# W2 = KV·Wo from full 128x128 array passes with a masked KV, plainer normalization, and four DMAs issued from ScalarE's queue

## The chip, the cores and the metric

The kernel runs on one core of a Trainium2 chip. The metric is device time in microseconds (us). TensorE (PE in the profile, with PEld for its weight loads) does the matrix products, VectorE (DVE) and ScalarE (ACT) empty PSUM and do the elementwise work, GpSimd (POOL) builds masks, and SyncE (SP) issues the DMAs. A DMA is issued from the instruction queue of one engine, and 16 DMA engines carry the data.

## The reference

The input x has 2048 rows of 1024 (bf16). Two attention blocks with 32 heads of 32 columns run on the same x, and a gate mixes them.

- Gate: g = sigmoid(sum of x * gate_w over a row).
- Block A is linear attention: q, k, v = x @ wqkv; phi(t) = (t + 1 where t > 0, else exp(t)) + 1e-6; per head KV = phi(k)^T v (32x32), z = the column sums of phi(k), and o = (phi(q) KV) / (phi(q)·z + 1e-6); a = o @ wo.
- Block B is sliding-window attention: eight keys per query at distance 0, 2, ..., 14, softmax over them, then @ its own wo.
- Output: g * a + (1 - g) * b.

## The kernel before, in words

Rows are handled in 16 tiles of 128 (`NB`), the 1024 columns in eight slabs of 128 (`KT`). TensorE's order is written out by hand for the whole kernel, VectorE's for the first stage; the other queues follow the order in which the code issues.

**Start.** SyncE issues, in this order: the DMA transpose of row tile 0 of x into `xT` (L95), the first two quarters of the weight half `WkA[0]` (L99, 256 KB each, slabs 0-1 and 2-3), the transpose of row tile 1 (L98), quarters three and four (L99), then 14 more transposes (L102) and the bulk loads of further weights and of x by rows. ScalarE's first instruction is the load of its activation table (L70). TensorE spins 36 small warm-up products (L158), then takes tile 0 with slabs 0-3, tile 1 with slabs 0-3, tile 0 with 4-5, tile 1 with 4-5, and so on, each as its quarter lands (L152).

**Stage 1.** pk = phi(x Wk) for 16 tiles and two column halves (L152, 256 products). Then G = x^T pk (L200, 256 products), so that KV^T = Wv^T G can be had without ever forming v (L220). L220 makes the transposed 64x64 diagonal blocks in pairs: array tiles 128x64, two side by side, 128 products of 64 columns; two bank-sized results are copied into `KVT`, which is 128 x 8 x 64. Only the 32x32 head blocks in it are used.

**W2 and V.** Next KV is folded into Wo, W2 = KV·Wo, in place in `WoA`. `w2_event(g, half)` (L246) uses the array as 32x32 tiles: 16 products of 512 columns, one per head of half g, into four banks, emptied by VectorE and ScalarE two each (L250). A bank then holds four heads that are four apart, so that the rows of W2 come out in a permuted head order. The four events are interleaved with the 64 products of the first four V tiles of block B (`v_units`, L258) at places 8, 20, 32 and 44. PSUM pool `ps_1` has six banks, which KV, W2, V and Q share in rotation.

**V and Q of block A.** Twelve rounds of 16 V products (L258) and 16 Q products of block A (L296). `qa_finish` applies phi and `normalize`: product with z (L277), sum per head (L279), + 1e-6 (L281), reciprocal (L282), times `ratio` (L284), and two multiplications of 512 columns that write the result in the same permuted head order as W2's rows (L286). The result goes to DRAM (`pqd`) and comes back transposed later.

**Stage 2** is block B: K and Q projections (L339) with scores (L365) and weighted sums (L390) interleaved. **Stage 3** multiplies: for each row tile, 8 slabs of normalized phi(q) with W2 and 8 slabs of block B's output with its Wo accumulate in one bank (L454); ScalarE scales it by 1 - g (`omg`, L459; W2's side carries the factor `ratio` = g/(1 - g)) and SyncE stores it (L461). Row tiles 12-15 are normalized late (`qa_late`), from `raw` into a tile of their own, `lw`. The last row tile is written in three parts of 512, 256 and 256 columns.

Of the kernel before, what the change touches and what calls it, by code (L numbers as in the profile page):

```python
# [9 lines left out]
ALU = mybir.AluOpType  # L10
BF16 = mybir.dt.bfloat16
F32 = mybir.dt.float32
PE = mybir.EngineType.PE
DVE = mybir.EngineType.DVE
P = 128
# [14 lines left out]
def interleave(units, events):  # L30

    events = sorted(events, key=lambda e: e[0])
    for i, unit in enumerate(units):
        while events and events[0][0] <= i:
            events.pop(0)[1]()
        unit()
    for _, fn in events:
        fn()
# [3 lines left out]
def kernel(  # L42
# [11 lines left out]
    nc = tc.nc  # L54
    S, D = A_x.shape[1:]
# [3 lines left out]
    out2 = out[0].rearrange("(m two) d -> two m d", two=2)  # L59

    def rows(ap, s0, s1):
        return ap[s0 // 1024, s0 % 1024:(s1 - 1) % 1024 + 1, :]

    H = 32
    Dh = D // H
    KT = D // P
    NB = S // P
# [4 lines left out]
    consts = ctx.enter_context(tc.tile_pool(name="consts", bufs=1))  # L72
    wpool = ctx.enter_context(tc.tile_pool(name="wpool", bufs=2))
# [20 lines left out]
    WkA = [wpool.tile([P, KT, 512], BF16, name="WkA0", tag="wa")]  # L94
    nc.sync.dma_start_transpose(out=xT[:, :, 0:P], in_=rows(x, 0, P))  # L95
    for i in range(4):
        if i == 2:
            nc.sync.dma_start_transpose(out=xT[:, :, P:2 * P], in_=rows(x, P, 2 * P))  # L98
        nc.sync.dma_start(out=WkA[0][:, 2 * i:2 * i + 2, :],  # L99
                          in_=A_wqkv[2 * i * P:(2 * i + 2) * P, D:D + 512].rearrange("(kt p) n -> p kt n", p=P))  # L100
    for t in range(2, NB):
        nc.sync.dma_start_transpose(out=xT[:, :, t * P:(t + 1) * P], in_=rows(x, t * P, (t + 1) * P))  # L102
    WkA += load_w("WkA", A_wqkv, D, "wa", only=(1,))
# [3 lines left out]
    WvA = load_w("WvA", A_wqkv, 2 * D, "wb")  # L107
    WoA = load_w("WoA", A_wo, 0, "wo")
# [3 lines left out]

    onesb = consts.tile([P, P], BF16, name="onesb")
    nc.vector.memset(onesb[:], 1.0)


    def band(dst, lead):
# [11 lines left out]
    ratio = consts.tile([P, NB], F32, name="ratio")  # L129
    omg = consts.tile([P, NB], F32, name="omg")  # L130
    zrow = consts.tile([P, D], F32, name="zrow")
    KVT = consts.tile([P, KT, 64], BF16, name="KVT")

    work = ctx.enter_context(tc.tile_pool(name="work", bufs=3))
    small3 = ctx.enter_context(tc.tile_pool(name="small3", bufs=2))
# [7 lines left out]
    with tc.manual_schedule(engines={PE}):  # L143

        with ExitStack() as s1:
            ps_1 = s1.enter_context(tc.tile_pool(name="ps_1", bufs=6, space=bass.MemoryType.PSUM))
# [37 lines left out]
            for t in range(1, NB):  # L184
                side.append(lambda t=t: nc.vector.tensor_tensor(
                    out=zacc[:], in0=zacc[:] if t > 1 else pk[:, 0, :], in1=pk[:, t, :], op=ALU.add))
            side.append(lambda: nc.gpsimd.partition_all_reduce(zrow[:], zacc[:], P, bass_isa.ReduceOp.add))
            for t in range(NB):
                side.append(lambda t=t: nc.vector.tensor_tensor_reduce(
                    out=gjunk[:], in0=xrow[:, t, :], in1=gw_row[:], scale=1.0, scalar=0.0, op0=ALU.mult,  # L190
                    op1=ALU.add, accum_out=gdot[:, t:t + 1]))

            G = []
            for half in range(2):
                g_ = kq.tile([P, KT, 512], BF16, name=f"G{half}", tag="kq")
                G.append(g_)
                for kt in range(KT):
                    pj = ps_1.tile([P, 512], F32, name="g_ps", tag="p1")
                    for t in range(NB):
                        nc.tensor.matmul(pj[:], lhsT=xrow[:, t, kt * P:(kt + 1) * P],  # L200
                                         rhs=pk[:, t, half * 512:(half + 1) * 512],
                                         start=(t == 0), stop=(t == NB - 1))
# [7 lines left out]
            nc.vector.tensor_scalar(out=omg[:], in0=ratio[:], scalar1=1.0, scalar2=None, op0=ALU.add)  # L210
            nc.vector.reciprocal(out=omg[:], in_=omg[:])


            for g in range(2):
                kvp = ps_1.tile([P, 4, 64], F32, name="kv_ps", tag="p1")
                for c in range(4):
                    for kt in range(KT):
                        for j in range(2):
                            cols = slice(c * P + 64 * j, c * P + 64 * j + 64)
                            nc.tensor.matmul(kvp[64 * j:64 * j + 64, c, :], lhsT=WvA[g][:, kt, cols],  # L220
                                             rhs=G[g][:, kt, cols], start=(kt == 0), stop=(kt == KT - 1))
                nc.vector.tensor_copy(out=KVT[:, 4 * g:4 * g + 4, :], in_=kvp[:])
            WkB = load_w("WkB", B_wqkv, D, "wb")


# [9 lines left out]
            def bank1():  # L235
                return ps_1.tile([P, 512], F32, name="p1_ps", tag="p1")

            def w2_event(g, half):  # L240
                def go():
                    w2p = [bank1() for _ in range(4)]
                    for j in range(4):
                        for r in range(4):
                            rs = slice(32 * r, 32 * r + 32)
                            nc.tensor.matmul(w2p[r][32 * j:32 * j + 32, :],  # L246
                                             lhsT=KVT[rs, 4 * g + j, (r % 2) * 32:(r % 2) * 32 + 32],
                                             rhs=WoA[half][rs, 4 * g + j, :], start=True, stop=True)
                    for r in range(4):
                        (nc.scalar.copy if r % 2 else nc.vector.tensor_copy)(  # L250
                            out=WoA[half][:, 4 * g + r, :], in_=w2p[r][:])
                return go

            def v_units(t):
# [21 lines left out]
            def normalize(t, pq, pn, prod):  # L276
                nc.vector.tensor_tensor(out=prod, in0=pq, in1=zrow[:], op=ALU.mult)  # L277
                den = small3.tile([P, H], F32, name="den", tag="den")
                nc.vector.tensor_reduce(out=den[:], in_=prod.rearrange("p (h e) -> p h e", h=H),  # L279
                                        axis=mybir.AxisListType.X, op=ALU.add)  # L280
                nc.vector.tensor_scalar(out=den[:], in0=den[:], scalar1=1e-6, scalar2=None, op0=ALU.add)  # L281
                nc.vector.reciprocal(out=den[:], in_=den[:])  # L282

                nc.vector.tensor_scalar(out=den[:], in0=den[:], scalar1=ratio[:, t:t + 1], scalar2=None, op0=ALU.mult)  # L284
                for g in range(2):
                    nc.vector.tensor_tensor(  # L286
                        out=pn[:, 512 * g:512 * g + 512].rearrange("p (r j e) -> p j r e", r=4, j=4),
                        in0=pq[:, 512 * g:512 * g + 512].rearrange("p (j r e) -> p j r e", r=4, j=4),
                        in1=den[:, 16 * g:16 * g + 16].rearrange("p (j r o) -> p j r o", r=4, o=1)
                        .broadcast_to([P, 4, 4, Dh]), op=ALU.mult)  # L290

            def qa_units(t, bank, evacuate):
                def mm(half, kt, st):
# [16 lines left out]
                    nc.sync.dma_start(out=pqd[t * P:(t + 1) * P, :], in_=pn)  # L310

            units = [u for t in range(4) for u in v_units(t)]
            interleave(units, [(8 + 12 * (2 * g + half), w2_event(g, half)) for g in range(2) for half in range(2)])
            for t in range(12):
                for u in v_units(4 + t):
                    u()
# [5 lines left out]
        with ExitStack() as s2:  # L322
# [102 lines left out]
            WoB = load_w("WoB", B_wo, 0, "wb")  # L425
            raw = wpool.tile([P, 4, D], BF16, name="raw", tag="wc")
            fw = wpool.tile([P, 2, D], F32, name="fw", tag="wc")
            lw = wpool.tile([P, 4, D], BF16, name="lw", tag="wa")
            pqT = [kq.tile([P, KT, 512], BF16, name="pqT0", tag="kq")]
            for t in range(4):  # L430
                nc.sync.dma_start_transpose(out=pqT[0][:, :, t * P:(t + 1) * P], in_=pqd[t * P:(t + 1) * P, :])
# [4 lines left out]
            def qa_late(t):  # L436
                r = raw[:, t - 12, :]
                for half in range(2):
                    h = slice(half * 512, (half + 1) * 512)
                    phi(r[:, h], r[:, h])  # L440
                pn = lw[:, t - 12, :]
                normalize(t, r, pn, fw[:, t % 2, :])
                nc.sync.dma_start_transpose(out=pqT[1][:, :, (t - 4) * P:(t - 3) * P], in_=pn)

            def out_units(tb, bank):
                def mm(c0, n, side, c, st):
                    if side == 0 and c == 0:
                        st["ps"] = bank()
                    if side == 0:
                        lhsT, W = (pqT[0][:, c, tb * P:(tb + 1) * P] if tb < 4 else  # L450
                                   pqT[1][:, c, (tb - 4) * P:(tb - 3) * P]), WoA
                    else:
                        lhsT, W = OBT[:, c, tb * P:(tb + 1) * P], WoB
                    nc.tensor.matmul(st["ps"][:, 0:n], lhsT=lhsT, rhs=W[c0 // 512][:, c, c0 % 512:c0 % 512 + n],  # L454
                                     start=(side == 0 and c == 0), stop=(side == 1 and c == KT - 1))
                    if side == 0 or c < KT - 1:
                        return
                    osb = work.tile([P, 512], BF16, name="osb", tag="e")
                    nc.scalar.activation(out=osb[:, 0:n], in_=st["ps"][:, 0:n], func=ACT.Copy,  # L459
                                         scale=omg[:, tb:tb + 1])  # L460
                    nc.sync.dma_start(out=rows(out2, tb * P, (tb + 1) * P)[:, c0:c0 + n], in_=osb[:, 0:n])  # L461
                parts = [(0, 512), (512, 512)] if tb < NB - 1 else [(0, 512), (512, 256), (768, 256)]
                for c0, n in parts:
                    st = {}
                    for side in range(2):
                        for c in range(KT):
                            yield lambda c0=c0, n=n, side=side, c=c, st=st: mm(c0, n, side, c, st)
# [51 lines left out]
```

## Time and profile before

| | |
|---|---|
| runs | 487.98 us median of 3 (487.95 to 489.38) |
| profiled execution | 487.95 us, its span 486.2 us |
| TensorE busy | 480.5 us, 99% of the span |
| VectorE busy | 281.0 us, 58% |
| ScalarE busy | 187.4 us, 39% |
| granted TensorE clock | 1.00 |
| DMA traffic | 46.57 MB; all 80144 program packets on one queue |

The span runs from the first to the last instruction in the trace; the run's time has some 1.7 us around it. An engine's busy time is the union of its instructions' intervals. Products of TensorE overlap in the records: each lasts longer than the distance to the next one, so the cost of a group is read from start to start, or from the chain of work that ended last, and not from the mean duration.

### The profile page before, as it was taken

To read this page: it belongs to the slowest core of one execution; us is meant where nothing else is said; L and a number is where in the kernel's file an instruction comes from. 1 tells how busy PE (TensorE), PEld (TensorE's weight loads), DVE (VectorE), ACT (ScalarE), POOL (GpSimd) and SP (SyncE) were. 2 spreads that over 40 slices of the span, in tenths; PEclk is the share of its full clock that TensorE was granted. 3 is DMA by queue.
4 is the path that set the end of the run, shared out by engine and by line. 5 is a ranking of instruction groups with operands and counts; after the bars stand their busy time and mean duration, and the time that the engine had idled before them with its cause. 6 is when DMAs were issued, how large, how long until landed. Compare 5 with 4: busy or idle time off the path is not lost.

```text
span 486.2 us, 8390 instructions
## 1 busy us (share of the span) xinstructions
PE 480.5 (99%) x3444; PEld 227.0 (47%) x3444; DVE 281.0 (58%) x533; ACT 187.4 (39%) x283; POOL 15.9 (3%) x33
## 2 busy tenths in 40 slices
PE   7999999999999999999999999999999999999997
PEld 4444444445444444444444445544445444444444
DVE  1766689992429999995466556656654596000000
ACT  1333321111633333332666666666565332212121
POOL 3000001411000000000000000000000000000000
PEclk9999999999999999999999999999999999999999
DMA  8999960001522223354011161111173833111101
GB/s 194 171 291 369 348 207 0 0 1 36 190 76 93 72 71 93 95 158 131 11 30 31 30 121 27 38 30 32 31 172 78 198 88 86 34 43 34 43 33 45
DMA packets 80182, 46.57 MB, mean 96 GB/s; under 512 B 53520, under 2 KB 74128, under 8 KB 80144
## 3 DMA queue, kind: packets, MB, share of 16 engines
q1 hardware_dynamic: 80144, 46.04, 34.9%
q8 instruction: 27, 0.44, 0.4%
q14 instruction: 11, 0.09, 0.1%
HBM read 21.23 MB, written 7.34 MB: 59 GB/s over the span
## 4 chain that ended last, share of the span: by engine, by line
PE 98%; DMA 1%; SPq 1%; ACT 0%; issue 0%; ACTq 0%
PE kq_ps L339 23%; PE d_ps L454 21%; PE p_ps L258 11%; PE g_ps L200 11%; PE pk_ps L152 11%; PE p_ps L296 9%; PE q_ps L296 3%; PE oB L390 3%; PE s L365 2%; PE q_ps L454 1%; DMA WkA<-in_A_wqkv_dram 1%; PE kv_ps L220 0%; PE p_ps L246 0%; SPq L95 0%; SPq L98 0%; SPq L99 0%
## 5 line engine op out<-in xcount | busy, mean ns | idle before, releaser
L375 ACT ACTIVATE PT<-s 128x896 bf16<-128x896 f32 (+1 forms) x72 | 63.0, 926 | 24.5 <-PE s L365 24.5
L339 PE MATMUL kq_ps<-xT,WkB 128*128 128x512 bf16 x256 | 65.3, 379 | 0.0
L339 PE MATMUL kq_ps<-xT,WqB 128*128 128x512 bf16 x256 | 64.8, 379 | 0.0
L376 DVE TENSOR_TENSOR PT<-PT,mask 128x896 bf16<-128x896 bf16 (+1 forms) x72 | 44.6, 623 | 26.6 <-ACT PT L375 26.6
L258 PE MATMUL p_ps<-WvB,xT 128*128 128x512 bf16 x256 | 57.9, 379 | 0.0
L152 PE MATMUL pk_ps<-WkA,xT 128*128 128x512 bf16 x256 | 56.0, 379 | 1.3 <-DMA WkA<-in_A_wqkv_dram 0.8
L454 PE MATMUL d_ps<-WoA,pqT 128*128 128x512 bf16 (+1 forms) x248 | 56.9, 372 | 0.0
L454 PE MATMUL d_ps<-WoB,OBT 128*128 128x512 bf16 (+1 forms) x248 | 56.9, 372 | 0.0
L200 PE MATMUL g_ps<-pk,xrow 128*128 128x512 bf16 x256 | 55.4, 379 | 0.0
L140 DVE TENSOR_SCALAR e<-e 128x512 f32<-128x512 f32 x64 | 28.1, 438 | 41.8 <-ACT e L139 41.8
L459 ACT ACTIVATE osb<-d_ps,omg 128x512 bf16<-128x512 f32 (+1 forms) x31 | 20.9, 673 | 76.5 <-PE d_ps L454 73.7
L296 PE MATMUL p_ps<-WqA,xT 128*128 128x512 bf16 x192 | 43.4, 379 | 0.0
L344 ACT CAST kqt<-kq_ps 128x512 bf16<-128x512 f32 x48 | 28.2, 587 | 31.8 <-PE kq_ps L339 31.6
L152 PEld LDWEIGHTS <-xT 128*128 128x128 bf16 x256 | 24.9, 98 | 32.2 <-issue 1.6
L454 PEld LDWEIGHTS <-pqT 128*128 128x128 bf16 x264 | 25.8, 98 | 29.5
L454 PEld LDWEIGHTS <-OBT 128*128 128x128 bf16 x264 | 25.8, 98 | 29.3
L200 PEld LDWEIGHTS <-xrow 128*128 128x128 bf16 x256 | 25.0, 98 | 30.2
L258 PEld LDWEIGHTS <-xT 128*128 128x128 bf16 x256 | 24.6, 98 | 30.0 <-issue 0.9
L296 PEld LDWEIGHTS <-xT 128*128 128x128 bf16 x256 | 24.3, 98 | 28.5
L139 ACT ACTIVATE e<-pk_ps 128x512 f32<-128x512 f32 x32 | 19.0, 597 | 42.0 <-PE pk_ps L152 42.0
L339 PEld LDWEIGHTS <-WqB 128*128 128x128 bf16 x256 | 22.9, 97 | 24.7
L339 PEld LDWEIGHTS <-WkB 128*128 128x128 bf16 x256 | 22.6, 97 | 24.1
(56 smaller groups left out, 394.1 us busy)
## 6 DMA issues: line engine op xcount, KB each, us to landing
xrow<-in_A_x_dram SPq DMA_DIRECT2D x4, 1024.0 KB, 12.3
out_dram<-osb SPq DMA_DIRECT2D x31, 128.0 KB, 1.9
pqd<-tmp SPq DMA_DIRECT2D x12, 256.0 KB, 2.0
WvA<-in_A_wqkv_dram SPq DMA_DIRECT2D x2, 1024.0 KB, 15.0
WoA<-in_A_wo_dram SPq DMA_DIRECT2D x2, 1024.0 KB, 12.7
WvB<-in_B_wqkv_dram SPq DMA_DIRECT2D x2, 1024.0 KB, 12.5
WqA<-in_A_wqkv_dram SPq DMA_DIRECT2D x2, 1024.0 KB, 9.7
WkB<-in_B_wqkv_dram SPq DMA_DIRECT2D x2, 1024.0 KB, 6.6
```

What stands on the lines that cost most here:

```text
L139: nc.scalar.activation(out=e[:], in_=pj[:], func=ACT.Exp)
L140: nc.vector.tensor_scalar(out=e[:], in0=e[:], scalar1=1.0, scalar2=1e-6, op0=ALU.min, op1=ALU.add)
L152: nc.tensor.matmul(pj[:], lhsT=xT[:, kt, t * P:(t + 1) * P], rhs=WkA[half][:, kt, :], start=(kt == 0), stop=(kt == KT - 1))
L200: nc.tensor.matmul(pj[:], lhsT=xrow[:, t, kt * P:(kt + 1) * P], rhs=pk[:, t, half * 512:(half + 1) * 512], start=(t == 0), stop=(t == NB - 1))
L258: nc.tensor.matmul(st["pj"][:], lhsT=xT[:, kt, t * P:(t + 1) * P], rhs=WvB[half][:, kt, :], start=(kt == 0), stop=(kt == KT - 1))
L296: nc.tensor.matmul(st["pj"][:], lhsT=xT[:, kt, t * P:(t + 1) * P], rhs=WqA[half][:, kt, :], start=(kt == 0), stop=(kt == KT - 1))
L339: nc.tensor.matmul(st["pj"][:], lhsT=W[c // 4][:, kt, (c % 4) * P:(c % 4 + 1) * P], rhs=xT[:, kt, cols], start=(kt == 0), stop=(kt == KT - 1))
L344: (nc.vector.tensor_copy if 0 <= after < 4 else nc.scalar.copy)(out=kqt[:, which, cols], in_=st["pj"][:])
L375: nc.scalar.activation(out=ptv[:, hs], in_=s4[:, hs, 0:W_], func=ACT.Exp, scale=SCALE)
L376: nc.vector.tensor_tensor(out=ptv[:, hs], in0=ptv[:, hs], in1=m[:, None, :].broadcast_to([P, 2, W_]), op=ALU.mult)
L454: nc.tensor.matmul(st["ps"][:, 0:n], lhsT=lhsT, rhs=W[c0 // 512][:, c, c0 % 512:c0 % 512 + n], start=(side == 0 and c == 0), stop=(side == ...
L459: nc.scalar.activation(out=osb[:, 0:n], in_=st["ps"][:, 0:n], func=ACT.Copy, scale=omg[:, tb:tb + 1])
```

## The change

**KV.** `KVT` becomes 128 x 8 x 128. For each of the eight slabs, eight full 128x128 products of 128 columns give the whole 128x128 block of Wv^T G, and one VectorE multiplication with a constant mask (`bdmask`, ones in the four 32x32 diagonal blocks) writes it to `KVT`.

**W2.** An event now belongs to a slab c: for each half of Wo one full 128x128 product of 512 columns, lhsT the masked block, emptied by VectorE (half 0) or ScalarE (half 1). Eight events, at places 4, 12, ..., 60 among the same 64 V products. W2's rows are in natural head order.

**Normalization.** `ratio` and the head's reciprocal are applied by one VectorE instruction over 1024 columns, in natural order. The late tiles are normalized in place in `raw`, and `lw` is gone.

**Queues.** The first quarter of `WkA[0]` is issued from ScalarE's queue, behind the table load, and the three stores of the last row tile from ScalarE's queue. In the built program the other instructions of all engines keep their order, and the five memsets of the mask stand behind that of `onesb` on VectorE.

```diff
-        nc.sync.dma_start(out=WkA[0][:, 2 * i:2 * i + 2, :],
-                          in_=A_wqkv[2 * i * P:(2 * i + 2) * P, D:D + 512].rearrange("(kt p) n -> p kt n", p=P))
+        (nc.sync if i else nc.scalar).dma_start(
+            out=WkA[0][:, 2 * i:2 * i + 2, :],
+            in_=A_wqkv[2 * i * P:(2 * i + 2) * P, D:D + 512].rearrange("(kt p) n -> p kt n", p=P))
...
+    bdmask = consts.tile([P, P], F32, name="bdmask")
+    nc.vector.memset(bdmask[:], 0.0)
+    for i in range(4):
+        nc.vector.memset(bdmask[32 * i:32 * i + 32, 32 * i:32 * i + 32], 1.0)
...
-    KVT = consts.tile([P, KT, 64], BF16, name="KVT")
+    KVT = consts.tile([P, KT, P], BF16, name="KVT")
...
-            for g in range(2):
-                kvp = ps_1.tile([P, 4, 64], F32, name="kv_ps", tag="p1")
-                for c in range(4):
-                    for kt in range(KT):
-                        for j in range(2):
-                            cols = slice(c * P + 64 * j, c * P + 64 * j + 64)
-                            nc.tensor.matmul(kvp[64 * j:64 * j + 64, c, :], lhsT=WvA[g][:, kt, cols],
-                                             rhs=G[g][:, kt, cols], start=(kt == 0), stop=(kt == KT - 1))
-                nc.vector.tensor_copy(out=KVT[:, 4 * g:4 * g + 4, :], in_=kvp[:])
+            for c in range(KT):
+                kvp = ps_1.tile([P, P], F32, name="kv_ps", tag="p1")
+                for kt in range(KT):
+                    nc.tensor.matmul(kvp[:], lhsT=WvA[c // 4][:, kt, (c % 4) * P:(c % 4 + 1) * P],
+                                     rhs=G[c // 4][:, kt, (c % 4) * P:(c % 4 + 1) * P],
+                                     start=(kt == 0), stop=(kt == KT - 1))
+                nc.vector.tensor_tensor(out=KVT[:, c, :], in0=kvp[:], in1=bdmask[:], op=ALU.mult)
...
-            def w2_event(g, half):
+            def w2_event(c):
                 def go():
-                    w2p = [bank1() for _ in range(4)]
-                    for j in range(4):
-                        for r in range(4):
-                            rs = slice(32 * r, 32 * r + 32)
-                            nc.tensor.matmul(w2p[r][32 * j:32 * j + 32, :],
-                                             lhsT=KVT[rs, 4 * g + j, (r % 2) * 32:(r % 2) * 32 + 32],
-                                             rhs=WoA[half][rs, 4 * g + j, :], start=True, stop=True)
-                    for r in range(4):
-                        (nc.scalar.copy if r % 2 else nc.vector.tensor_copy)(
-                            out=WoA[half][:, 4 * g + r, :], in_=w2p[r][:])
+                    for half in range(2):
+                        w2p = bank1()
+                        nc.tensor.matmul(w2p[:], lhsT=KVT[:, c, :], rhs=WoA[half][:, c, :], start=True, stop=True)
+                        if half:
+                            nc.scalar.copy(out=WoA[half][:, c, :], in_=w2p[:])
+                        else:
+                            nc.vector.tensor_copy(out=WoA[half][:, c, :], in_=w2p[:])
                 return go
...
-                nc.vector.tensor_scalar(out=den[:], in0=den[:], scalar1=ratio[:, t:t + 1], scalar2=None, op0=ALU.mult)
-                for g in range(2):
-                    nc.vector.tensor_tensor(
-                        out=pn[:, 512 * g:512 * g + 512].rearrange("p (r j e) -> p j r e", r=4, j=4),
-                        in0=pq[:, 512 * g:512 * g + 512].rearrange("p (j r e) -> p j r e", r=4, j=4),
-                        in1=den[:, 16 * g:16 * g + 16].rearrange("p (j r o) -> p j r o", r=4, o=1)
-                        .broadcast_to([P, 4, 4, Dh]), op=ALU.mult)
+                nc.vector.scalar_tensor_tensor(
+                    out=pn.rearrange("p (h e) -> p h e", h=H), in0=pq.rearrange("p (h e) -> p h e", h=H),
+                    scalar=ratio[:, t:t + 1], in1=den[:].rearrange("p (h o) -> p h o", o=1).broadcast_to([P, H, Dh]),
+                    op0=ALU.mult, op1=ALU.mult)
...
-            interleave(units, [(8 + 12 * (2 * g + half), w2_event(g, half)) for g in range(2) for half in range(2)])
+            interleave(units, [(4 + 8 * c, w2_event(c)) for c in range(KT)])
...
-            lw = wpool.tile([P, 4, D], BF16, name="lw", tag="wa")
...
-                pn = lw[:, t - 12, :]
-                normalize(t, r, pn, fw[:, t % 2, :])
-                nc.sync.dma_start_transpose(out=pqT[1][:, :, (t - 4) * P:(t - 3) * P], in_=pn)
+                normalize(t, r, r, fw[:, t % 2, :])
+                nc.sync.dma_start_transpose(out=pqT[1][:, :, (t - 4) * P:(t - 3) * P], in_=r)
...
-                    nc.sync.dma_start(out=rows(out2, tb * P, (tb + 1) * P)[:, c0:c0 + n], in_=osb[:, 0:n])
+                    (nc.sync if tb < NB - 1 else nc.scalar).dma_start(
+                        out=rows(out2, tb * P, (tb + 1) * P)[:, c0:c0 + n], in_=osb[:, 0:n])
```

## The prediction

> **What bounds the kernel now.** I read the page's shares first, then the chain that ended last in order of time, then the timelines of the stretches that the change touches.
>
> ```profile
> PE 480.5 (99%) x3444; PEld 227.0 (47%) x3444; DVE 281.0 (58%) x533; ACT 187.4 (39%) x283; POOL 15.9 (3%) x33
> PE 98%; DMA 1%; SPq 1%; ACT 0%; issue 0%; ACTq 0%
> 170.00:180.00 10.00, 10.00 (x48) 4.56 (x47) 9.62 (x16) 3.56 (x6) 0.00 (x0) 1.00 0.26 86
> ```
>
> TensorE is the chain from end to end. The third line is one stretch of the rounds in which VectorE is fullest (columns: length, then busy PE, PEld, DVE, ACT, POOL, clock, DMA): VectorE has 9.62 of 10.00 us, and TensorE still loses nothing. So a change counts only by what it does to TensorE's own time, to the start (the first 8.69 us), or to the tail behind the last product. The chain, in order of time (start, length, what), at the start and around KV and W2:
>
> ```profile
> 2.20 0.56 SPq L99
> 2.76 0.05 issue
> 2.82 0.46 SPq L99
> 3.27 0.04 issue
> 3.31 1.25 SPq L98
> 4.57 0.04 issue
> 4.61 4.03 DMA WkA<-in_A_wqkv_dram
> 8.64 0.04 issue
> 8.69 53.74 PE pk_ps L152 x248
> ...
> 117.69 2.15 PE kv_ps L220 x128
> 119.83 1.83 PE p_ps L258 x8
> 121.66 0.36 PE p_ps L246 x16
> 122.03 2.70 PE p_ps L258 x12
> ```
>
> Until 8.69 us the chain is SyncE issuing one DMA after another and the third weight quarter landing. Later, 128 array-tile products cost 2.15 us and 16 packed ones 0.36 us: the packing that the change gives up. TensorE's timeline gives the rates (start, union, line, count):
>
> ```profile
> 5.78 0.59 PE L152 MATMUL pk_ps<-WkA,xT 128*128 128x512 bf16 x2 [0.64 <-DMA WkA<-in_A_wqkv_dram]
> 6.58 0.59 PE L152 MATMUL pk_ps<-WkA,xT 128*128 128x512 bf16 x2 [0.21 <-DMA WkA<-in_A_wqkv_dram]
> 7.60 2.76 PE L152 MATMUL pk_ps<-WkA,xT 128*128 128x512 bf16 x11 [0.43 <-DMA xT<-in_A_x_dram]
> ...
> 475.81 1.89 PE L454 MATMUL d_ps<-WoA,pqT 128*128 128x512 bf16 x8
> 477.54 1.89 PE L454 MATMUL d_ps<-WoB,OBT 128*128 128x512 bf16 x8
> 479.27 1.04 PE L454 MATMUL d_ps<-WoA,pqT 128*128 128x256 bf16 x8
> 480.14 1.04 PE L454 MATMUL d_ps<-WoB,OBT 128*128 128x256 bf16 x8
> ```
>
> From start to start, eight products of 512 columns take 1.73 us (215.8 ns each) and eight of 256 take 0.87 us (109.1 ns each). Half the columns save 106.7 ns, so a product costs 0.417 ns per column plus 2.4 ns.
>
> **KV and W2 on TensorE.** The chain's piece from 117.69 to 139.09 us holds L220, the four L246 events and 80 V products (8 + 12 + 12 + 12 + 36). It is 21.40 us; 80 x 0.2158 = 17.26 us are V, so KV, W2 and the switches of array mode around them cost 4.14 us. (By starts: KV 2.24 us, each event 0.46 us, of which some 0.1 us is the switch.) After the change the array stays in one mode. KV is 64 products of 128 columns; no such product at full clock is in the trace. By the line above it is 53.3 + 2.4 = 55.8 ns. From below it can't go under the columns' own 53.3 ns; from above, a weight load that doesn't hide adds its pace, for which the weighted sums are the row: 16 products of 33 columns, each with a 128x128 weight load, take 0.40 us on the chain, 24.7 ns a pair, hence at most 80 ns. I take 55.8, because the 256-column row shows the same kind of load hidden. 64 x 55.8 = 3.57 us (3.41 to 5.13). W2 is 16 products of 512 columns: 16 x 215.8 = 3.45 us. Together 7.02 us against 4.14: **+2.88 us**, all on the path, since TensorE does nothing else meanwhile.
>
> The Trainium skill ("TensorE: Matmul & The Clock Gate", Part 2, Back-to-back issue gap) speaks harder against this change: in a stream of load and product pairs it gives about 81 ns per product of 128 columns. That would make KV 5.18 us and the sum +4.5 us. The same passage gives 131 ns at 512 columns, where this trace has 215.8, so I let the rows decide.
>
> **What lies beside it, at nothing.** The eight masked multiplications replace two copies of 424 ns; at 128 columns each is no dearer than that, while eight products of KV last 0.446 us, and the waits put VectorE idle 7.8 us before the first copy. If that cover went, slab 0 would be first needed four V products (0.86 us) after KV ends, later slabs 2.16 us apart. W2's evacuations keep their number and size (8 x 686 ns on VectorE, 8 x 594 ns on ScalarE); per event and eight V products, 2.16 us, each engine has at most 1.18 us to do, and three of six banks are taken, so TensorE finds a free one. WkB's load waits for WvA, freed some 1.3 us later; it lands 6.6 us after issue and is wanted at 218.5 us. The mask's five memsets (nearest row: 165 ns each) fall between 1.1 us and VectorE's next work at 10.8 us. The normalization loses 241 + 2 x 688 ns and gains one instruction over 1024 columns; the nearest rows (1225 ns for a 1024-column multiplication, twice 692 ns for this operation at 512) put it at 1.2 to 1.4 us. That is 0.2 to 0.4 us less VectorE work in each of 16 tiles, and nothing of it on the path, by the 10.00 of 10.00 above. Dropping `lw` removes no wait that TensorE shows.
>
> **The start.** On ScalarE's queue the first quarter stands behind the table load (0.80 to 2.08 us), so it is issued at about the old time (2.20 us) at the latest, or earlier if the queue runs ahead of the load. What moves is everything behind it on SyncE: the second quarter, tile 1's transpose and the third quarter go out 0.62 us earlier (2.82 less 2.20). The third quarter's landing ends the chain. From above: if all data were there when the warm-up ends (about 4.93 us), eight products (1.73 us) would bring TensorE to 6.66 instead of 8.69 us, a gain of 2.0 us. The queue's slot allows 0.62 us of it directly. From below: the DMA engines are at 0.85 in the first 12.15 us, so an earlier issue may only wait there; the gain is then nothing, and with two queues taking turns the second quarter could delay the first. That delay has slack (the first could be used 1.1 us later without moving 8.69), so I put the loss at 0.3 us at most. I take a gain of **0.5 us**, a little under the slot, since the engines aren't quite idle.
>
> The Trainium skill ("Perfetto Trace Analysis", DMA Instruction — HWDGE) says that descriptor generation is one block, locked by the sequencer that uses it. Then ScalarE's issue would only wait its turn against SyncE's, the gain would be about nothing and the total 490.9; the trace has a single issuing queue and can't show it.
>
> **The tail.** Of the three stores moved to ScalarE, two are issued (0.33 us each) in ScalarE's 1.06 and 1.27 us waits for TensorE. The last one is issued by SyncE 26 ns after the activation ends; ScalarE could do it that much sooner, or later by a similar hop. I take 0, bounds -0.1 and +0.1 us. Nothing else stands behind them on either queue.
>
> **Sum.** 2.88 - 0.5 + 0 = +2.4 us. The profiled execution took 487.95 us (486.2 of span and 1.75 around it), which is the median 487.98 to 0.03 us; 487.98 + 2.4 = **490.4 us**, with the span at 488.6.
>
> **Rivals.**
> - *Weight loads bind KV* (80 ns a product): for it, no 128-column product at full clock is on show; against it, 24.7 ns a pair at 33 columns and loads fully hidden at 256. 64 x 24.2 ns = +1.5 us: 491.9 us.
> - *The start gains nothing*, the transfer being bound by the DMA engines: for it, the 0.85 share and quarters and transposes landing about 0.8 to 1.1 us apart; against it, the first quarter was used only at 5.78 us, over 3 us after its issue, while tile 1's transpose was still unissued. 490.9 us, or 491.2 with the 0.3 us loss.
> - *Not slower* (within 0.3%): the start gains so much that it pays for W2. It needs 1.42 us, that is, TensorE in steady flow at 7.27 us or sooner. The ceiling is 2.0, so it is possible, but the issue moves by 0.62 only. If ScalarE issues at 0.8 us, ahead of the first transpose's data, the third quarter is one transfer (0.8 us) sooner, not two. At a gain of 1.6 us: 489.3 us.
> - *VectorE's relief pays*: it would need a TensorE wait in the V and Q rounds, and there is none; faster than before would take more than the 2.0 us that the start has.
>
> **How the numbers follow.** The forecast (gain of 0.2 to 0.9 us at the start, KV near 56 ns) 0.55; no gain or a loss at the start 0.25; weight loads bind 0.08; not slower 0.09; faster by any way 0.03. A change under 0.3% (1.46 us) counts as none for this kernel. The first three cases are all slower (490.0 us and up): 0.88; same 0.09; faster 0.03. The range goes from 489.6 us (a start gain of 1.3) to 491.3 us (no start gain, a little of the weight loads showing).
>
> **What would show it.** Right: L220's 64 products about 56 ns apart, 3.6 us in all; 16 products of W2 at 216 ns with no gaps around them; 117.7 to 139.1 grown by 2.9 us; the third quarter's products starting near 8.2 us instead of 8.69; VectorE some 5 us less busy and PE still at 99%. Wrong: KV products 80 ns apart; a TensorE wait on `KVT` or for a bank; the third quarter at 8.6 us or later, or below 7.3; a tail longer than the present 3.2 us from the last activation's start to the end of the span.

## The result and the profile after

The changed kernel took 490.98 us (median of 6 runs, 490.68 to 491.8) against 488.53 us of the kernel before in the same comparison (6 runs): a ratio of 1.0049, with a 95% interval of 1.0032 to 1.0066, or +2.4 us. The forecast was 490.4 us, +2.4 us. The profiled execution took 491.39 us, 0.4 us over its median, with a span of 489.7 us.

The page of the changed kernel, busy times and the chain by engine:

```profile
PE 483.1 (99%) x3332; PEld 229.5 (47%) x3332; DVE 279.1 (57%) x512; ACT 188.0 (38%) x283; POOL 16.3 (3%) x33
PE 92%; SPq 5%; DMA 2%; issue 0%; ACT 0%
```

TensorE is still the bound. That the chain now has 5% of SyncE's queue isn't a new bound in itself: at the start it leads through one more wait, shown below. The chain of the changed kernel around KV and W2 (start, length, what):

```profile
118.26 3.57 PE kv_ps L221 x64
121.84 0.86 PE p_ps L255 x4
122.70 0.43 PE p_ps L244 x2
123.13 1.73 PE p_ps L255 x8
124.86 0.43 PE p_ps L244 x2
...
138.24 4.32 PE p_ps L255 x20
142.56 0.65 PE p_ps L289 x3
```

KV is 64 products in 3.57 us, 55.8 ns each; each W2 event is two products in 0.43 us with nothing around it, since the array keeps one mode. From KV's start to the first Q product (L289) it is 142.56 - 118.26 = 24.30 us, where it was 21.40: +2.90 us, against +2.88 in the forecast.

TensorE's timeline at the start and around the second half of the first weight (start, union, line, count, and the wait ahead of the row):

```profile
4.65 0.61 PE L157 MATMUL pk_ps<-WkA,xT 128*128 128x512 bf16 x2
6.13 0.59 PE L157 MATMUL pk_ps<-WkA,xT 128*128 128x512 bf16 x2 [0.87 <-DMA WkA<-in_A_wqkv_dram]
7.26 1.04 PE L157 MATMUL pk_ps<-WkA,xT 128*128 128x512 bf16 x4 [0.54 <-DMA xT<-in_A_x_dram]
...
8.53 26.16 PE L157 MATMUL pk_ps<-WkA,xT 128*128 128x512 bf16 x120 [0.23 <-DMA WkA<-in_A_wqkv_dram]
35.21 27.80 PE L157 MATMUL pk_ps<-WkA,xT 128*128 128x512 bf16 x128 [0.52 <-DMA WkA<-in_A_wqkv_dram]
```

The first quarter is used at 4.65 us instead of 5.78, but the third at 8.53 instead of 8.69 us: in this execution 1.1 us gained at the first product are 0.16 by the ninth. Then, before product 129, which has the second weight half as its operand, stands a wait that the kernel before didn't have. From start to start of the products it costs 0.68 us more than a full pace.

The account of the two profiled executions, by the chains: up to KV's start 117.69 became 118.26 (+0.57: 0.16 gained at the ninth product, 0.72 lost in waits after it, nearly all of it before product 129); KV to the first Q product +2.90; from there to the end of the last product 343.84 in both; the tail behind the last product 3.2 us in both. Together that is the 3.5 us between the spans.

ScalarE's and SyncE's queues at the start, two timelines of the changed kernel:

```profile
0.79 1.28 ACT L70 ACT_TABLE_LOAD   x1 [0.79 <-PEq L495]
0.83 0.44 ACTq L99 DMA_DIRECT2D WkA<-in_A_wqkv_dram  x1
```

```profile
0.80 1.34 SPq L95 DMA_TRANSPOSE xT<-in_A_x_dram  x1
2.20 0.56 SPq L99 DMA_DIRECT2D WkA<-in_A_wqkv_dram  x1
2.82 1.25 SPq L98 DMA_TRANSPOSE xT<-in_A_x_dram  x1
4.11 1.09 SPq L99 DMA_DIRECT2D WkA<-in_A_wqkv_dram  x2
```

ScalarE issued at 0.83 us, not behind the table load, and its 0.44 us ran beside SyncE's first transpose, which took the same 1.34 us as before. What is left on SyncE moved by 0.50 us for the third quarter (4.61 to 4.11).

And VectorE, groups of the changed kernel (line, operation, shapes and count; busy us and mean ns of one; idle before):

```profile
L280 DVE SCALAR_TENSOR_TENSOR tmp<-tmp,ratio,den 128x1024 bf16<-128x1024 bf16 x12 | 15.4, 1285 | 0.4
L224 DVE TENSOR_TENSOR KVT<-kv_ps,bdmask 128x128 bf16<-128x128 f32 x8 | 2.3, 291 | 8.2 <-PE kv_ps L221 8.2
```

The new normalization step takes 1285 ns in place of 241 + 2 x 688, so 0.33 us less per tile. The masking takes 291 ns beside 446 ns of products, and VectorE waits for TensorE there, not the other way.

### The profile page after: what moved, and what is told of

Its sections match the earlier page's. It is cut to its first block, busy times and chain, and to the rows that moved or that the text cites. A ratio compares the mean times of both kernels' runs of the same rounds, so it can differ in the third digit from the quotient of the medians.

```text
span 489.7 us, 8140 instructions
## 1 busy us (share of the span) xinstructions
PE 483.1 (99%) x3332; PEld 229.5 (47%) x3332; DVE 279.1 (57%) x512; ACT 188.0 (38%) x283; POOL 16.3 (3%) x33
## 4 chain that ended last, share of the span: by engine, by line
PE 92%; SPq 5%; DMA 2%; issue 0%; ACT 0%
PE kq_ps L332 23%; PE d_ps L445 21%; PE g_ps L205 11%; PE p_ps L255 11%; PE p_ps L289 8%; PE pk_ps L157 6%; SPq L103 4%; PE q_ps L289 3%; PE oB L383 3%; PE s L358 2%; DMA WkA<-in_A_wqkv_dram 2%; PE q_ps L445 1%; PE kv_ps L221 1%; PE p_ps L244 1%; SPq L99 0%; SPq L95 0%
## 5 line engine op out<-in xcount | busy, mean ns | idle before, releaser
L289 PE MATMUL p_ps<-WqA,xT 128*128 128x512 bf16 x192 | 43.4, 379 | 0.0
L289 PEld LDWEIGHTS <-xT 128*128 128x128 bf16 x256 | 24.3, 98 | 28.5
## 6 DMA issues: line engine op xcount, KB each, us to landing
WoA<-in_A_wo_dram SPq DMA_DIRECT2D x2, 1024.0 KB, 12.2
```

What stands on the lines that cost most here:

```text
L289: nc.tensor.matmul(st["pj"][:], lhsT=xT[:, kt, t * P:(t + 1) * P], rhs=WqA[half][:, kt, :], start=(kt == 0), stop=(kt == KT - 1))
```

## The experiments

Each was run together with the kernel before, in four comparisons on two chips; ratios are to the runs of that kernel in the same comparison, whose median went from 488.17 to 488.94 us. Two questions were open after the result: whether the two parts of the sum are each right, and what the first quarter's queue really did.

**KV alone, W2 alone.** The first kernel is that of before with the full KV products:

```diff
+            for c in range(KT):
+                kvp = ps_1.tile([P, P], F32, name="kv_ps", tag="p1")
+                for kt in range(KT):
+                    nc.tensor.matmul(kvp[:], lhsT=WvA[c // 4][:, kt, (c % 4) * P:(c % 4 + 1) * P],
+                                     rhs=G[c // 4][:, kt, (c % 4) * P:(c % 4 + 1) * P],
+                                     start=(kt == 0), stop=(kt == KT - 1))
+                nc.vector.tensor_tensor(out=KVT[:, c, :], in0=kvp[:], in1=bdmask[:], op=ALU.mult)
...
-                                             lhsT=KVT[rs, 4 * g + j, (r % 2) * 32:(r % 2) * 32 + 32],
+                                             lhsT=KVT[rs, 4 * g + j, rs],
```

> The kernel before with KV alone from full products and the mask; W2 stays in 32x32 array tiles and reads the diagonal blocks of the wider KVT. By the forecast's sum KV goes from 2.24 to 3.57 us: the stretch from the start of KV to the first Q product grows from 21.40 to 22.7 us, the total by 1.3 us, a ratio of 1.0027. If the array's mode switches cost more than the 0.1 us that I gave each, the growth is smaller, since one switch between KV and V goes.

The second is the changed kernel with the paired 128x64 products back:

```diff
-                nc.vector.tensor_tensor(out=KVT[:, c, :], in0=kvp[:], in1=bdmask[:], op=ALU.mult)
...
+                for j in range(2):
+                    r = slice(64 * j, 64 * j + 64)
+                    nc.vector.tensor_tensor(out=KVT[r, 4 * g:4 * g + 4, r], in0=kvp[r],
+                                            in1=bdmask[r, None, r].broadcast_to([64, 4, 64]), op=ALU.mult)
```

> The changed kernel with KV alone in pairs of 128x64 array tiles again, masked into KVT by four instructions on 64 partitions (KVT cleared once at the start); W2 as full products. By the forecast's sum W2 goes from four events of 0.46 us to 3.45 us and KV stays at 2.24 us: the stretch is 21.40 + 1.6 = 23.0 us. In time: theory A, +1.3 to +1.7 us over before by chance of the start; theory B, +2.1 us, with the wait before product 129 again, since the first quarter stays on ScalarE's queue.

Measured: 489.54 us, ratio 1.0024 (1.0013 to 1.0035), and 489.65 us, ratio 1.0023 (1.0012 to 1.0034). Their chains, first KV alone, then W2 alone:

```profile
117.96 3.57 PE kv_ps L221 x64
121.53 1.73 PE p_ps L260 x8
123.26 0.36 PE p_ps L248 x16
123.62 2.70 PE p_ps L260 x12
...
140.68 1.51 PE p_ps L298 x7
```

```profile
117.73 2.15 PE kv_ps L225 x128
119.88 0.97 PE p_ps L261 x4
120.85 0.43 PE p_ps L250 x2
121.28 1.73 PE p_ps L261 x8
...
140.71 1.29 PE p_ps L295 x6
```

The stretch is 140.68 - 117.96 = 22.72 us (+1.32, forecast +1.33) with KV alone and 140.71 - 117.73 = 22.98 us (+1.58, forecast +1.61) with W2 alone. They add up to the 2.90 of both. In the second kernel's profile the wait before product 129 did not come back, though its first quarter is on ScalarE's queue, too; so that wait is not a fixed price of the queue. It stands in two more profiles below: 0.44 us in the timeline of the kernel with the old normalization, with the quarter on ScalarE's queue, and 0.57 us in that of the longer warm-up, with the quarter on SyncE's.

**The normalization.**

```diff
-                nc.vector.scalar_tensor_tensor(
-                    out=pn.rearrange("p (h e) -> p h e", h=H), in0=pq.rearrange("p (h e) -> p h e", h=H),
-                    scalar=ratio[:, t:t + 1], in1=den[:].rearrange("p (h o) -> p h o", o=1).broadcast_to([P, H, Dh]),
-                    op0=ALU.mult, op1=ALU.mult)
+                nc.vector.tensor_scalar(out=den[:], in0=den[:], scalar1=ratio[:, t:t + 1], scalar2=None, op0=ALU.mult)
+                for g in range(2):
+                    nc.vector.tensor_tensor(
+                        out=pn[:, 512 * g:512 * g + 512].rearrange("p (h e) -> p h e", h=16),
+                        in0=pq[:, 512 * g:512 * g + 512].rearrange("p (h e) -> p h e", h=16),
+                        in1=den[:, 16 * g:16 * g + 16].rearrange("p (h o) -> p h o", o=1)
+                        .broadcast_to([P, 16, Dh]), op=ALU.mult)
```

> The changed kernel with the normalization's last step as three instructions again (times ratio, then two multiplications of 512 columns), in natural head order. VectorE gets 0.2 to 0.4 us more work in each of 16 tiles, 5 us in all; TensorE never waits for it, the stretch from KV to the first Q product stays 24.3 us, the rounds of V and Q keep 6.91 us each, and the time is that of the changed kernel, a ratio of 1.005 to before.

Measured: 490.69 us, ratio 1.0042 (1.0025 to 1.0059), no slower than the changed kernel. VectorE's busy time rose from 279.1 to 283.2 us, and the stretch from KV to the first Q product stayed 24.3 us. VectorE's relief is worth nothing here.

**The first quarter's queue, undone and alone.**

```diff
-        (nc.sync if i else nc.scalar).dma_start(
+        nc.sync.dma_start(
```

> The changed kernel with the first weight quarter issued from SyncE again; everything else as changed. Theory A (the early quarter is worth only the 0.16 us that the third quarter's products started sooner, and the 0.68 us wait for the second weight half before product 129 is chance in the DMA engines, not the queue's doing): the third quarter's products start at about 8.7 us, the median is within 0.3% of the changed kernel, +2.5 to +3.0 us over before, and a wait before product 129 can appear or not. Theory B (the early quarter makes the second weight half late): no such wait, KV starts at 117.7 us, and the kernel is 0.5 us faster than the changed one, about +1.9 to +2.3 us over before. In both the stretch from the start of KV to the first Q product is 24.3 us.

Alone, in the kernel before, with the stores:

```diff
-        nc.sync.dma_start(out=WkA[0][:, 2 * i:2 * i + 2, :],
+        (nc.sync if i else nc.scalar).dma_start(out=WkA[0][:, 2 * i:2 * i + 2, :],
...
-                    nc.sync.dma_start(out=rows(out2, tb * P, (tb + 1) * P)[:, c0:c0 + n], in_=osb[:, 0:n])
+                    (nc.sync if tb < NB - 1 else nc.scalar).dma_start(out=rows(out2, tb * P, (tb + 1) * P)[:, c0:c0 + n], in_=osb[:, 0:n])
```

> The kernel before with the two queue edits alone: first weight quarter and the last row tile's three stores from ScalarE's queue. Theory A: the third quarter's products start at about 8.5 instead of 8.69 us, the tail is unchanged at 3.2 us, the time is that of before to 0.2 us or so, a ratio of 0.9995 to 1.000. Theory B: the second weight half lands about 1 us later, TensorE waits 0.7 us before product 129, and the time is 0.5 us over before. The forecast as written had a gain of 0.5 us here, a ratio of 0.999.

Measured: undone 491.71 us, ratio 1.0056 (1.0043 to 1.007); alone 488.05 us, ratio 0.999 (0.998 to 0.9999). Theory B falls: taking the early quarter away made the kernel no faster. (1.0056 against 1.0049 for the changed kernel, with intervals that overlap, doesn't show it slower either.) Alone, the gain of 0.1%, 0.5 us, is the forecast's size, though its interval nearly touches 1. But the profiles show something that the forecast had not named. The timeline of the kernel with the quarter moved back:

```profile
5.85 1.86 PE L157 MATMUL pk_ps<-WkA,xT 128*128 128x512 bf16 x4 [0.71 <-DMA WkA<-in_A_wqkv_dram]
7.92 6.43 PE L157 MATMUL pk_ps<-WkA,xT 128*128 128x512 bf16 x24 [0.20 <-DMA xT<-in_A_x_dram]
```

Four products in 1.86 us are at half pace (in the changed kernel four take 1.04): here the clock records give full speed only from 10.1 us on. And the kernel with the queue edits alone, by timeline and in stretches (length; busy PE, PEld, DVE, ACT, POOL; granted clock; DMA):

```profile
7.11 0.59 PE L152 MATMUL pk_ps<-WkA,xT 128*128 128x512 bf16 x2 [1.33 <-DMA WkA<-in_A_wqkv_dram]
8.24 5.96 PE L152 MATMUL pk_ps<-WkA,xT 128*128 128x512 bf16 x19 [0.54 <-DMA xT<-in_A_x_dram]
```

```profile
4.00:8.00 4.00, 2.37 (x15) 1.31 (x13) 0.00 (x0) 0.00 (x0) 0.00 (x0) 1.00 1.16 175
8.00:12.00 4.00, 3.76 (x11) 1.43 (x12) 0.00 (x0) 0.00 (x0) 2.80 (x14) 0.60 1.08 256
```

Its clock was granted in full at 5.4 us, taken back at 8.8 and given again at 12.2. This execution, 489.98 us, is the slowest of its twelve; the others are 487.83 to 488.85 us. So two things come out differently from execution to execution: when full clock is granted in the first 12 us, and how late the second weight half lands. The runs of the kernel before show it as well: of the 30 in the comparison of the next group, 19 are at 487.7 to 488.7 us, one at 489.0 and ten at 489.3 to 490.2.

**The two chances apart.** The second weight half in four quarters, so that product 129 needs only the first of them:

```diff
-    WkA += load_w("WkA", A_wqkv, D, "wa", only=(1,))
+    WkA.append(wpool.tile([P, KT, 512], BF16, name="WkA1", tag="wa"))
+    for i in range(4):
+        nc.sync.dma_start(out=WkA[1][:, 2 * i:2 * i + 2, :],
+                          in_=A_wqkv[2 * i * P:(2 * i + 2) * P, D + 512:D + 1024].rearrange("(kt p) n -> p kt n", p=P))
```

> The kernel before, with the second weight half (wanted at 34.6 us, landed at 34.0 us in its profile and 1.2 us later in the changed kernel's) loaded in four quarters instead of one DMA. If its late landing is a part of the spread between runs, no wait stands before product 129, the slowest runs go (before: up to 490.0 us) and the median falls by some 0.2 to 0.4 us, a ratio of 0.9992 to 0.9996. If the spread comes from the granted clock in the first 12 us alone (full speed began at 5.8 us in the profile of before, at 10.1 in that of the first quarter moved back, and fell away from 8.8 to 12.2 in that of the queues alone), the ratio is 1.000 and the slow runs stay.

Measured: 487.93 us, ratio 0.9993 (0.9977 to 1.001). Seven of twelve runs are at 487.64 to 487.96 us and five at 489.13 to 490.95. No wait stands before product 129 in its profile, but the clock came late in it (489.16 us, full speed from 10.5 us).

The same load with the first quarter on ScalarE's queue:

```diff
-        nc.sync.dma_start(out=WkA[0][:, 2 * i:2 * i + 2, :],
+        (nc.sync if i else nc.scalar).dma_start(out=WkA[0][:, 2 * i:2 * i + 2, :],
```

> The same, and the first weight quarter from ScalarE's queue; stores untouched. By the median of the queues alone (ratio 0.999) it takes 488.1 us, ratio 0.9985 to 0.999; TensorE's first products start at 4.65 to 4.95 us instead of 5.8. If the gain of the queues was chance, the ratio is that of the quarters of the second half without it.

Measured: 487.7 us, ratio 0.9978 (0.9967 to 0.9989). Eleven runs are within 487.25 and 488.03 us; the twelfth, 2833.51 us, is a disturbed execution and left out. This kernel keeps the packed products, and it beats both the kernel before and the changed one.

The rival for the gain is that TensorE, fed at 4.9 us, is simply not idle after the warm-up. It was tested without any early quarter, by a longer warm-up:

```diff
-            warm_up(36)
+            warm_up(45)
```

> The kernel before with 45 instead of 36 warm-up products and nothing else: at 107 ns each they fill TensorE's wait of 0.9 us between the warm-up and the first weight quarter (used at 5.8 us). Theory C: the gain of issuing the first quarter early is that TensorE doesn't fall idle after the warm-up, so that full speed is granted by about 6.5 us at the latest; the runs of before fall into two groups (20 of 30 at 487.7 to 488.7, 10 at 489.0 to 490.2), and the slow group is the late clock. Then here too the slow group goes, the fastest runs stay at 487.7, the median falls by 0.3 to 0.6 us (ratio 0.9985 to 0.9995) with the third quarter's products still at 8.7 us. Rival D: the gain is the earlier landing of the quarters; then the slow group stays and the ratio is 1.000.

Measured: 488.15 us, ratio 0.9992 (0.998 to 1.0004), two of twelve runs over 488.5. In the profiled one, the slowest at 489.04 us, full clock came at 4.4 us and the time went to waits for tile 1's transpose (0.90 us in its timeline) and before product 129 (0.74 us from start to start). That left theory C undecided, since the second chance was still in it. Both measures together:

> The kernel before with the second weight half in four quarters and 45 warm-up products; the first quarter stays on SyncE's queue. With the quarters alone 5 of 12 runs were at 489.1 us or more, and the profiled one of them had full clock only from 10.5 us. With the first quarter on ScalarE's queue as well, none was over 488.03 us. Theory C (TensorE's idle 0.9 us after the warm-up is what lets the clock come late): no run over 488.5 us, full speed from 6.6 us or sooner, median 487.7 to 487.9, ratio near 0.998 to 0.999. Rival D (the earlier landing of the quarter is the gain): a third or more of the runs stay at 489 us or more.

Measured: 488.16 us, ratio 0.9983 (0.9973 to 0.9992), all twelve runs at 487.71 to 488.54 us, while eight of the 17 runs of the kernel before beside them were at 489.1 us or more. The two kernels differ in nine warm-up products only; stretches of TensorE's start, first with 36 of them, then with 45:

```profile
6.00:8.00 2.00, 1.73 (x5) 0.30 (x4) 0.00 (x0) 0.00 (x0) 0.00 (x0) 1.00 1.14 230
8.00:10.00 2.00, 2.00 (x5) 0.71 (x6) 0.00 (x0) 0.00 (x0) 1.42 (x6) 1.00 1.21 309
```

```profile
6.00:8.00 2.00, 1.17 (x4) 0.27 (x3) 0.00 (x0) 0.00 (x0) 0.00 (x0) 1.00 1.13 227
8.00:10.00 2.00, 1.94 (x9) 0.90 (x10) 0.00 (x0) 0.00 (x0) 1.58 (x8) 1.00 1.19 309
```

With TensorE full from 8 to 10 us, five products are half speed and nine are full speed (the clock column reads 1.00 in both: no record stands ahead of the first grant, and a stretch without a record reads as full). The two kernels were measured in different comparisons, on different chips; beside the first, 10 of 30 runs of the kernel before were late, beside the second 8 of 17. So theory C holds for the group of late runs: with the second half in quarters, closing the gap after the warm-up (from about 4.93 to 5.78 us) does away with it. Its forecast median, 487.7 to 487.9, was not reached, and one run is at 488.54.

The kernel with the early quarter stays about 0.5 us below this one. That is of the size of the difference between two comparisons, but the profiles point to a worth of the earlier quarters themselves. In the five executions with the first quarter on ScalarE's queue and full clock by then (the changed kernel, W2 alone, the old normalization, and, with the second half in quarters, the packed and the changed kernel) the ninth product starts at 8.01 to 8.79 us, 8.49 on average; in the four with it on SyncE's queue (the kernel before, KV alone, and both with 45 warm-up products) at 8.69 to 8.99, on average 8.89. These are few executions, and the two ranges overlap.

Filling the other waits of the start with warm-up products, on top of quarters and ScalarE's queue:

```diff
-            for t, kts in ((0, (0, 1, 2, 3)), (1, (0, 1, 2, 3)), (0, (4, 5)), (1, (4, 5)), (0, (6, 7)), (1, (6, 7))):
+            for t, kts, n in ((0, (0, 1), 12), (0, (2, 3), 8), (1, (0, 1, 2, 3), 4), (0, (4, 5), 0), (1, (4, 5), 0),
+                              (0, (6, 7), 0), (1, (6, 7), 0)):
                 for kt in kts:
                     project(first[t], t, kt, 0)
+                warm_up(n)
```

> The same, and 24 more warm-up products laid into the waits between the first weight quarters (12 after the first, 8 after the second, 4 after tile 1's slabs 0 to 3), so that TensorE is busy there. Theory of the clock: a granted clock that is chance because TensorE idles 1 to 2 us in its first 9 us; then the profile shows full speed from 4 to 6 us on without a fall, the runs lie within 0.5 us of each other and the median is 0.3 to 0.7 us below the kernel with the same loads and no filling. If the clock has nothing to do with the idle time, the filling costs up to 0.3 us where a quarter lands before it is through.

Measured: 488.14 us, ratio 0.9992 (0.9982 to 1.0002), all runs within 487.8 and 488.55. The spread is small, but the median is 0.4 us above the kernel without the filling, not below it: there was nothing left for it to gain. Where the 0.4 us go is not shown; in the two profiles KV starts 0.24 us later with the filling (117.93 against 117.69).

Two quarters on ScalarE's queue, the first and the third:

```diff
-        nc.sync.dma_start(out=WkA[0][:, 2 * i:2 * i + 2, :],
+        (nc.sync if i % 2 else nc.scalar).dma_start(out=WkA[0][:, 2 * i:2 * i + 2, :],
```

> The kernel before with the second weight half in four quarters, and the first and the third quarter of the first half from ScalarE's queue. The third quarter, whose landing ends the start's chain, goes out at 1.3 us instead of 4.6 and shares the DMA engines with the first transpose and the second quarter, which then land up to 0.8 us later. If the start is bound by the bytes that the DMA engines carry, steady flow still begins at 8.3 to 8.7 us and the time is that of the kernel with the first quarter alone on ScalarE's queue, 487.7 us, ratio 0.998; if it is bound by the order of issue, it begins near 7.9 us and the time is 487.1 us.

Measured: 488.95 us, ratio 1.0009 (0.9998 to 1.0021), slower than both of the forecast's cases. The first product waits for the first transpose until 6.58 us (in the kernel before TensorE loads from it at 4.83), and the ninth starts at 8.97 us:

```profile
6.58 1.07 PE L155 MATMUL pk_ps<-WkA,xT 128*128 128x512 bf16 x4 [1.44 <-DMA xT<-in_A_x_dram]
8.09 30.18 PE L155 MATMUL pk_ps<-WkA,xT 128*128 128x512 bf16 x136 [0.45 <-DMA xT<-in_A_x_dram]
```

So the third quarter out 3.3 us earlier doesn't start the ninth product sooner; the transposes land later instead, which speaks for a start that is bound by the bytes. And TensorE has a gap behind its warm-up again, 1.44 us in the timeline: eight of the twelve runs are at 488.87 us or more, four at 487.77 to 488.02. With the second half in quarters, that makes 13 late runs of 24 in the two kernels with a gap behind the warm-up (this one and the quarters alone) and none of 35 over 488.55 us in the three without (early quarter, filling, longer warm-up); the disturbed one is not counted. That is the best evidence for theory C, and it speaks against ScalarE's queue itself as the cure: this kernel uses it and has the late runs. It is not free of a rival, since here the transposes land late too, and the one execution profiled is among the fast four, with full clock at 5.4 us.

**The changed kernel with the second half in quarters** (the same edit as above):

> The changed kernel with the second weight half in four quarters. The wait of 0.68 us before product 129 in its profile can't stand here; KV starts at 117.5 to 117.9 us and the time falls from 490.98 to 490.5 us or a little under, ratio 1.004 to 1.005: the 2.9 us of KV and W2 over the best kernel with the same loads (487.7 us).

Measured: 490.72 us, ratio 1.0043 (1.0028 to 1.0059), KV's start at 117.7 us. Against 487.7 us for the packed kernel with the same loads and the same quarter on ScalarE's queue that is 3.0 us, the 2.9 us of KV and W2 and 0.1 beside. (The two stand in different comparisons; by their ratios, 1.0043 and 0.9978, it is 3.2 us.)

## Why the prediction was right

*KV and W2.* The term +2.88 measured +2.90, and its two parts came out alone (+1.32 and +1.58). The price for a product of 128 columns, drawn from rows of 512 and 256 columns, was 55.8 ns and is 55.8 ns; the mode switches went as booked. The rival of weight loads that don't hide (80 ns) is refuted by the 3.57 us of KV, and so is the figure of 81 ns in the Trainium skill ("TensorE: Matmul & The Clock Gate", Part 2, Back-to-back issue gap) for this stream, in which every product has its own 128x128 load.

*What was costed at nothing* cost nothing: masking, evacuations, WkB's load, the memsets, VectorE's relief (0.33 us per tile, within 0.2 to 0.4) and the tail (3.2 us before and after).

*The start.* The size, a gain of 0.5 us, agrees with the queue edits alone (0.1%, 0.0 to 0.2%); that it does is in part luck. In the changed kernel's profiled execution the third quarter's products, forecast near 8.2 us, started at 8.53, 0.16 us sooner than before, and the 0.50 us by which SyncE's queue moved was mostly lost to waiting on transfers. Over the few executions compared above the step is worth some 0.4 us, so it is neither refuted nor well measured. Two readings behind it were off. The share of 0.85 for the DMA engines in the first 12.15 us is an average over an empty beginning and a full rest; the kernel before in two stretches (the last two numbers are DMA share and GB/s; packets count where they start, so a share can pass 1):

```profile
0.00:4.00 4.00, 2.88 (x28) 2.89 (x29) 0.17 (x1) 1.28 (x1) 0.67 (x7) 1.00 0.36 73
4.00:8.00 4.00, 2.72 (x17) 1.47 (x16) 0.00 (x0) 0.00 (x0) 0.00 (x0) 1.00 1.06 286
```

And tile 1's transpose was not "still unissued" at 5.78 us: it was issued from 3.31 us on, while the first quarter was under way. Both speak for the rival of a start bound by the DMA engines, more than the prediction allowed.

What the early quarter does besides is to close the gap of some 0.9 us in which TensorE sits idle after its warm-up. That this idle time brings the late runs is supported by the counts above (13 of 24 with a gap, none of 35 without). How the clock goes with it is seen in the profiled executions: full clock came at 10.1 and 10.5 us in two of the five with the gap, at 3.9 to 5.8 in the other three, and at 4.0 to 6.6 in all nine without it (0.43 us in one with the longer warm-up counted as none). For most of the late runs that weren't profiled it is argued; each run's mean granted clock, though, says something. It is 0.997 in the execution whose clock was taken back for 3.4 us, and 0.996 or 0.997 in 26 of 139 runs of kernels with the gap against 3 of 89 without. (A late first grant leaves no such mark: the two executions that had it read 1.000.)

The forecast had no term for the clock, nor for the second weight half, whose landing at 34.0 us left 0.6 us to spare in the profile of before; both were read from a single execution as if they were fixed. The total fits in the medians; in the two profiled executions alone it would not have, for there the start lost 0.57 us where 0.5 were to be gained.

*The shared descriptor generation.* The Trainium skill ("Perfetto Trace Analysis", DMA Instruction — HWDGE) would have ScalarE's issue wait its turn. In this trace 0.44 us of ScalarE's issuing lie inside SyncE's 1.34 us, and neither got longer. Where the page and this differ, the measurement decides.

## What to carry to other kernels

Where one engine is the chain from end to end, price a change by that engine's start-to-start rates, from two sizes in the same trace, and add what stands around a switch of array mode; the sum for KV and W2 came out to 0.02 us. Look at how much a landing has to spare before you take a start as fixed, and split a load whose first part is wanted first. A warm-up should reach until the data are there: nine more products, with the split load, left no late run among twelve (alone they gained nothing clear of noise, ratio 0.9992). Before a landing or a clock from one profile goes into a sum, see how it varies over several executions.

## What the runs showed of the hardware that I had not expected

- Full clock is granted at 3.9 to 10.5 us after the start in the profiled executions, and in one of them was taken back for 3.4 us (8.8 to 12.2 us) around waits of 1.33 and 0.54 us; the three executions with a late grant or a fall took 1.18 to 2.15 us more than the fastest run of their kernel. The fall is not rare: a mean granted clock of 0.997, as that execution has, stands beside 18 of the 99 runs of the kernel before in the experiments.
- The issue of a DMA that stands behind a table load of 1.28 us in ScalarE's program starts 0.04 us after the load does (0.83 and 0.79 us), beside SyncE's issue of a transpose (0.80 to 2.14 us).
- Switching the array between 128x128 and smaller tiles costs about 0.1 us each time: behind KV, eight V products take 1.83 us on the chain of the kernel before, with a switch, and 1.73 us in that of full KV products, without one; behind a 32x32 event, twelve take 2.70 us, where twelve at 215.8 ns would take 2.59.
